# Attention decode over a cached K and V: the V loads move from SyncE's DMA queue to ScalarE's

## The chip, the cores and the metric

The kernel runs on one core of one Trainium2 chip. Five engines of the core follow their own instruction streams and meet through semaphores: TensorE (PE; its weight loads are shown as PEld), VectorE (DVE), ScalarE (ACT), GpSimd (POOL) and SyncE (SP). Transfers between HBM and the on-chip memory SBUF run on 16 DMA engines. An engine issues a transfer onto its own DMA queue and goes on; the transfer raises a semaphore when it has landed. The metric is the device time of one execution in microseconds (us), lower is better.

## The reference

One token per sequence (two sequences, D = 512) passes a block that adds a gated attention to its input. Only the parts that carry the time are kept here:

```python
xn = _layernorm(x)
q = (xn @ wq).reshape(B, 1, 32, 128)                 # 32 query heads
k = repeat(k_cache, 4, axis=1)                       # caches: (2, 8, 32768, 128), float32
v = repeat(v_cache, 4, axis=1)
p = softmax(einsum("bhqd,bhkd->bhqk", q, k) * 128 ** -0.5)
s = einsum("bhqk,bhkd->bhqd", p, v).reshape(B, 1, 4096) @ wo
gate, up = xn @ W_gate, xn @ W_up                    # 512 x 1792
g = silu(((gate * (gate > 0)) * up) @ W_down)
return x + s * g
```

K and V are 268 MB each, and every byte of them is read once. All arithmetic is float32.

## The kernel before

The 16 groups (a sequence and one of its 8 K/V heads, with 4 query heads each) have 32768 tokens each. A tile `t` is 8192 tokens, four tiles make a group, and two tiles make a pair. There are 64 tiles and 32 pairs (`PAIRS`). One transfer brings one pair of K or of V: 128 partitions of 64 KB, 8.39 MB.

Three large buffers of SBUF hold everything that is loaded. `kbuf[0]` and `kbuf[1]` (`k0`, `k1`) take the K pairs in turn. `wide` (shown as `w`) takes first `wq`, then the gate and up weights, then the down weights, and then one V pair after the other. So K is held twice and V once. At the end the V of pair 30 goes to `k0`, and `wo` to `k1` in six pieces.

The main loop (line 882) runs over steps `j` from 0 to 33. In step `j`

- DVE turns the K of pair `j` in place, in eight instructions (`k_transpose`, L660), and PE follows it with the scores (`scores`, tile `s`);
- PE sums the V of pair `j - 2` with its softmax weights (`values`, tile `o`);
- DVE takes the scores out of PSUM (`take_scores`, L678);
- in an odd step a group ends: its maximum is found and ScalarE takes the exponentials of its four tiles (`maximum`, L722); the group two steps back is divided by its sum and stored (`sums`, `take_o`, `finish_group`);
- PE and DVE bring the weights of pair `j - 1` into the layout for the next step's sums (`weights`, tile `pt`, and `take_weights`, L737);
- last, the step's loads are issued: the V of pair `j - 1`, then the K of pair `j + 2`.

All loads but two tiny ones go through `load` (L239) on SyncE, in this order, so its queue holds V, K, V, K in turn. The order of an engine's instructions is the order in which the program is written. `Program.op` works out the waits from the keys that an operation reads and writes: a load has to wait until the last reader of its buffer is done. For a V load that is the `values` call of the same step; for a K load it is the `scores` call of the same step. SyncE meets the V load first, so the K load behind it is issued when the sums over V are done too, although its own buffer is free since the scores.

ScalarE, VectorE and TensorE run the steps from 4 to 64 tiles as a hardware loop whose body is four tiles long (`looped`, L86); a body has to be the same in all rounds. ScalarE's body holds the four exponentials. SyncE's and GpSimd's programs are written out.

Of the kernel before, what the change touches and what calls it, by code (L numbers as in the profile page):

```python
# [162 lines left out]
def decode_block_kernel(nc, x, kc, vc, wq, wo, wg, wu, wd, out):  # L163
# [5 lines left out]
    NU = SK // TK  # L169
    NG = B * HKV  # L170
    NK = NG * NU
# [5 lines left out]
    PAIRS = NK // 2  # L177

    pg = Program()

    def sbuf(name, *shape, align=32):
        return nc.alloc_sbuf_tensor(name, list(shape), F32, align_bytes=align)[:]
# [5 lines left out]
    wide = sbuf("w", P, 2 * NC * NR * DH, align=ALIGN)  # L188
# [47 lines left out]
    def pe(fn, r=(), w=()):  # L236
        pg.op("PE", fn, r, w)

    def load(dst, src, sem, r=(), w=(), engine="SP"):  # L239
        pg.op(engine, lambda e: e.dma_start(dst, src), r, w, dma=sem)  # L240

    def mm(out_, lhs, rhs, start, stop):
        return lambda e: e.matmul(out_, lhs, rhs, start=start, stop=stop, skip_group_check=True)  # L243

    def chain(parts):
        def emit(e):
            for f in parts:
                got = f(e)
            return got

        return emit

    def group(g):
        return g % B, g // B
# [42 lines left out]
    for kb in range(4):  # L297
        dve(
            lambda e, kb=kb: e.memset(block_of[Q * kb : Q * kb + Q, kb * REP : (kb + 1) * REP], 1.0),
            w=["block_of"],  # L300
# [105 lines left out]
    def k_keys(b):  # L406
        return [f"k{b}"] + [f"k{b}_{i}_{c}" for i in range(2) for c in range(NC)]

    def load_kk(j):
        b = j % 2  # L410
        load(kbuf[b], rows_of(kc, 2 * j), f"k{b}", w=k_keys(b))

    def rows_of(src, t):
        b, hk = group(t // NU)
        lo = (t % NU) // 2 * 2 * TK
        return src[b, hk, lo : lo + 2 * TK, :].rearrange("(p r) d -> p (r d)", p=P)
# [6 lines left out]
    def place(t):  # L423
        if t in (NK - 4, NK - 3):
            return half_of(kbuf[0], t), "k0"
        return half_of(wide, t), "wide"

    def load_vv(j):
        if 2 * j == NK - 4:
            load(kbuf[0], rows_of(vc, 2 * j), "k0", w=k_keys(0))  # L430
        else:
            load(wide, rows_of(vc, 2 * j), "v", w=["wide"])

    def in_halves(tokens):
        return tokens.rearrange("p (h c r d) -> p h c r d", h=2, c=NC, d=DH)
# [3 lines left out]
    def load_wo():  # L439
        for quad, cuts in enumerate(((0, 16), (0, 8, 12, 14, 15, 16))):  # L440
            dst = kbuf[1][:, quad * ROWS * D : (quad + 1) * ROWS * D]
            WO.append(dst.rearrange("p (j d) -> p j d", j=ROWS))
            n = ROWS * P
            rows = wo[quad * n : (quad + 1) * n, :].rearrange("(p j) d -> p (j d)", j=ROWS)
            for lo, hi in zip(cuts, cuts[1:]):
                name = f"wo{quad}_{lo}"
                for j in range(lo, hi):
                    WOK[quad, j] = name
                load(
                    dst[:, lo * D : hi * D],  # L450
                    rows[:, lo * D : hi * D],
                    name,
                    w=[*k_keys(1), name] if quad == 0 else [name],
                )
# [71 lines left out]
    def take_query(g):  # L526
        b, hk = group(g)
        pg.op(
            "POOL",
            lambda e: e.tensor_tensor(  # L530
                qcur.rearrange("p e (k h) -> p e k h", h=REP),
                qall[:, b, hk].unsqueeze(2).to_broadcast([P, 4, Q // REP, REP]),
                block_of.rearrange("p (k h) -> p k h", h=REP)
                .unsqueeze(1)
                .to_broadcast([P, 4, Q // REP, REP]),
                op=ALU.mult,
            ),
            ["qall", "block_of"],
            ["qcur", "pool"],
        )  # L540
# [61 lines left out]
    def load_d():  # L602
        load(
            wide[:, : FI * D],
            wd.rearrange("(p i) d -> p (i d)", p=P),
            "wd",
            w=["wide", "wide_g", "wide_u"],
        )

    def mlp_down():  # L610
        ht = wt[1][:, : FI * Q].rearrange("p (i m) -> p i m", m=Q)
        pe(
            chain(
                [
                    mm(
                        ps_d[32 * (i % 4) : 32 * (i % 4) + 32, :],
                        ht[:, i, :],
                        wdt[:, i, :],
                        i < 4,
                        i >= FI - 4,  # L620
                    )
                    for i in range(FI)
                ]
            ),
            ["wt1", "wide"],
            ["d"],
        )
# [29 lines left out]
    def k_transpose(t, c):  # L657
        at_, key = turned(t, c)
        at_ = at_.rearrange("p h r d -> p h (r d)")
        dve(lambda e: e.transpose(at_, at_), [f"k{t // 2 % 2}"], [key])  # L660

    def scores(t):
        ps = ps_s[t % 2]

        def one(e, c):
            part = turned(t, c)[0].rearrange("p h r (e k) -> p h r e k", e=4)
            return mm(ps[Q * c : Q * c + Q, :], qcur[:, e, :], part[:, :, :, e, :], e == 0, e == 3)

        for c in range(NC):
            pe(one(0, c), [turned(t, c)[1], "qcur"], [f"s{t % 2}"])  # L670
        pe(chain([one(e, c) for e in (1, 2) for c in range(NC)]), ["qcur"], [f"s{t % 2}"])
        for c in range(NC):
            pe(one(3, c), [turned(t, c)[1], "qcur"], [f"s{t % 2}"])
# [62 lines left out]
    def take_weights(t):  # L736
        dve(lambda e: e.transpose(wt[t % 2], ps_p[t % 2]), [f"pt{t % 2}"], [f"wt{t % 2}"])  # L737

    def values(t):
        u = t % NU  # L740
        at_, key = place(t)
        w = wt[t % 2].rearrange("p (r m) -> p r m", m=Q)

        def one(r):
            a = Q * (r % 4)
            return mm(
                o_ps[a : a + NC * REP, :].rearrange("p (c d) -> p c d", c=NC),
                w[:, r, : NC * REP],
                in_halves(at_)[:, r // 8, :, r % 8, :],
                u == 0 and r < 4,  # L750
                u == NU - 1 and r >= NR - 4,
            )

        pe(chain([one(r) for r in range(NR)]), [f"wt{t % 2}", key], ["o"])
# [93 lines left out]
    def project_far():  # L848
# [25 lines left out]
            ["gy"],  # L874
        )

    load_kk(0)
    project_q()
    load_gu()
# [2 lines left out]
    for j in range(PAIRS + 2):  # L882
        s, v = 2 * j, 2 * (j - 2)
        pg.step = s
        live, summed, ends = j < PAIRS, v >= 0, j % 2
        if live:
            for t in (s, s + 1):
                for c in range(NC):
                    k_transpose(t, c)
                scores(t)  # L890
                if t == 2:
                    mlp_down()
            if ends and j + 1 < PAIRS:
                take_query(j // 2 + 1)
        if j == 0:
            mlp_gu("g", 0)
            mlp_gu("u", 1)
        if summed:
            values(v)
            values(v + 1)  # L900
        if live:
            take_scores(s)
            take_scores(s + 1)
        if j == 0:
            mlp_vector()
        if j == 1:
            mlp_fold()
        if ends:
            if live:
                tile_maximum()  # L910
            if summed:
                sums()
            if live:
                maximum()
            if summed:
                take_o()
                if not live:
                    project_near(range(2))
                finish_group(j // 2 - 1)
        if 0 <= v + 2 < NK:  # L920
            for t in (v + 2, v + 3):
                weights(t)
                take_weights(t)
        if j == 0:
            load_d()
        elif j < PAIRS - 1:
            load_vv(j - 1)
        if j == PAIRS - 2:
            load_vv(PAIRS - 2)
        if j + 2 < PAIRS:  # L930
            load_kk(j + 2)
        if j == PAIRS - 1:
            load_vv(PAIRS - 1)
            load_wo()

    project_near(range(2, NEAR))
    project_far()
# [2 lines left out]
    sems = {s: nc.alloc_semaphore(f"sem_{s}") for s in pg.count}  # L940
    with nc.Block(no_gpsimd_drain=True) as block:

        @block.sync
        def _(e):
            pg.emit("SP", e, sems)

        @block.scalar
        def _(e):
            pg.emit("ACT", e, sems, loop=(NU, NK))

        @block.gpsimd
        def _(e):
            pg.emit("POOL", e, sems)

        @block.vector
        def _(e):
            pg.emit("DVE", e, sems, loop=(NU, NK))

        @block.tensor
        def _(e):  # L960
            pg.emit("PE", e, sems, loop=(NU, NK))
# [34 lines left out]
```

## Time and profile before

| | before |
|---|---|
| median of 3 runs | 1309.91 us (1309.86 to 1310.29) |
| span of the profiled execution, first to last instruction | 1308.4 us |
| read from HBM | 564.67 MB, 432 GB/s over the span |
| TensorE busy | 859.0 us (66%) |
| VectorE busy | 718.1 us (55%) |
| ScalarE busy | 51.4 us (4%) |
| transfers of K and V | 32 + 32, of 8.39 MB |

The median is 1.5 us above the span of the profiled execution. A row of the timeline gives start, duration, engine, line, operation, output and input, and in brackets how long the engine had been idle and what ended that. `SPq` and `ACTq` are the DMA queues' issuing instructions. A row by windows gives, for a stretch of time, the busy time of each engine, then the clock that TensorE was granted, the mean busy share of the 16 DMA engines, and the rate in GB/s.

### The profile page before, as it was taken

The page shows a single profiled execution, that of the slowest core. Times are in us where ns is not written, and L with a number is a line of the kernel's source. Part 1 is how long each engine was busy: PE and PEld are TensorE (multiplying, and loading weights), DVE is VectorE, ACT ScalarE, POOL GpSimd, SP SyncE. Part 2 cuts the span into 40 slices and gives each one's busy share as a digit, 9 for nine tenths or more (in the row PEclk, how much of TensorE's full clock was granted, in tenths as well). Part 3 has the DMA queues.
Part 4 walks back from the last instruction along what each step waited for, and adds up shares of the span by engine and source line. Part 5 has one row for each costly group of instructions (what it writes and reads, how often), then busy time and mean ns, then how long its engine had stood idle before and what let it go on. Part 6 is the DMA issues. An engine that isn't in the chain of part 4 may idle for free.

```text
span 1308.4 us, 11146 instructions
## 1 busy us (share of the span) xinstructions
PE 859.0 (66%) x4720; PEld 211.5 (16%) x4720; DVE 718.1 (55%) x690; ACT 51.4 (4%) x133; POOL 10.5 (1%) x38
## 2 busy tenths in 40 slices
PE   3566675785666587576667667667665757865676
PEld 1111111211111121111111112121111112111121
DVE  3566654565655456664546666455665545656521
ACT  0001000000000000000000000000000000000000
POOL 0000000000000000000000000000000000000000
PEclk9677788878878887878898778798887889788788
DMA  9999999999999999999999999999999999999998
GB/s 417 423 438 435 437 431 441 425 439 429 437 429 439 435 433 441 429 441 427 439 429 437 429 439 435 433 441 429 441 427 439 429 437 429 439 435 433 439 431 357
DMA packets 10693, 564.79 MB, mean 432 GB/s; under 512 B 1195, under 2 KB 1211, under 8 KB 1597
## 3 DMA queue, kind: packets, MB, share of 16 engines
q1 hardware_dynamic: 10668, 564.67, 99.7%
q8 instruction: 6, 0.10, 0.0%
q14 instruction: 3, 0.02, 0.0%
q10 hardware_dynamic: 16, 0.01, 0.0%
HBM read 564.67 MB, written 0.00 MB: 432 GB/s over the span
## 4 chain that ended last, share of the span: by engine, by line
DMA 64%; DVE 17%; PE 15%; issue 4%; SPq 0%
DMA k<-in_A_k_cache_dram 58%; DVE k L660 17%; PE o L243 8%; PE s L243 6%; DMA k<-in_A_wo_dram 3%; DMA w<-in_A_wq_dram 2%; PE m_ps L243 1%; PE m_ps L693 0%; PE d L243 0%; SPq L240 0%; DVE gy L870 0%; DVE gy L872 0%
## 5 line engine op out<-in xcount | busy, mean ns | idle before, releaser
L243 PE MATMUL s<-k,qcur 128*32 128x512 f32 x2048 | 504.5, 710 | 370.5 <-DVE k L660 370.3
L660 DVE STREAM_TRANSPOSE k<-k 128x2048 f32<-128x2048 f32 x256 | 565.2, 2275 | 147.0 <-DMA k<-in_A_k_cache_dram 147.0
L243 PE MATMUL o<-w,wt 128*16 128x512 f32 x1984 | 245.5, 596 | 9.0 <-DMA w<-in_A_v_cache_dram 9.0
L243 PEld LDWEIGHTS s<-k,qcur 128*32 128x32 f32 x2048 | 89.5, 123 | 785.0 <-DVE k L660 639.3
L737 DVE STREAM_TRANSPOSE wt<-pt 128x512 f32<-128x512 f32 x64 | 45.9, 717 | 139.4 <-PE pt L243 134.6
L678 DVE TENSOR_SCALAR_CACHE_REDUCE st<-s 128x512 f32<-128x512 f32 x64 | 43.0, 672 | 120.9 <-PE s L243 120.9
L243 PEld LDWEIGHTS o<-w,wt 128*16 128x16 f32 x1984 | 62.4, 98 | 167.5 <-issue 167.5
L722 ACT ACTIVATE st<-st,nb 128x512 f32<-128x512 f32 x64 | 45.4, 710 | 1111.0 <-DVE nb L719 1111.0
L243 PE MATMUL pt<-st,perm 128*128 128x512 f32 x128 | 72.6, 696 | 1.5 <-ACT st L722 1.5
L763 DVE RECIPROCAL rl<-m_ps 128x1 f32<-128x1 f32 x16 | 2.7, 169 | 111.0 <-PE m_ps L243 111.0
L243 PE MATMUL m_ps<-ob,heads 128*128 128x128 f32 x128 | 21.7, 321 | 29.0 <-DVE ob L777 29.0
L243 PEld LDWEIGHTS pt<-st,perm 128*128 128x128 f32 x128 | 25.3, 219 | 34.4 <-issue 30.1
L803 DVE STREAM_TRANSPOSE os<-m_ps 128x512 f32<-128x512 f32 x16 | 11.5, 717 | 23.2 <-PE m_ps L243 23.2
L243 PEld LDWEIGHTS m_ps<-ob,heads 128*128 128x128 f32 x128 | 18.0, 217 | 31.1 <-DVE ob L777 31.1
L243 PE MATMUL m_ps<-w,wt 128*32 128x512 f32 (+1 forms) x128 | 16.2, 640 | 8.1 <-DMA w<-in_A_wq_dram 8.1
L777 DVE SCALAR_TENSOR_TENSOR ob<-o,share,ob 128x128 f32<-128x128 f32 x48 | 16.9, 351 | 1.7
L530 POOL TENSOR_TENSOR qcur<-qall,block_of 128x128 f32<-128x128 f32 x16 | 6.5, 406 | 1008.3 <-PE s L243 974.0
L243 PE MATMUL m_ps<-negone,mrow 1*128 1x1 f32 x32 | 6.0, 256 | 9.3 <-DVE mrow L708 9.3
L722 ACT ACTIVATION_READ_ACCUMULATOR st<-st,nb 128x1 f32 x64 | 11.9, 186 | 0.0
L481 DVE COPY os<-m_ps 128x512 f32<-128x512 f32 x2 | 1.4, 692 | 16.3 <-PE m_ps L243 16.3
L243 PE MATMUL o<-k,wt 128*16 128x512 f32 x64 | 8.4, 687 | 2.8 <-DMA k<-in_A_v_cache_dram 2.8
L391 PE MATMUL m_ps<-ident,st 32*128 32x32 f32 x4 | 0.7, 307 | 14.0 <-DVE st L380 14.0
(80 smaller groups left out, 102.8 us busy)
## 6 DMA issues: line engine op xcount, KB each, us to landing
k<-in_A_wo_dram SPq DMA_DIRECT2D x1, 4096.0 KB, 37.3
w<-in_B_W_gate_dram SPq DMA_DIRECT2D x1, 3584.0 KB, 19.6
w<-in_B_W_up_dram SPq DMA_DIRECT2D x1, 3584.0 KB, 27.6
w<-in_B_W_down_dram SPq DMA_DIRECT2D x1, 3584.0 KB, 15.6
k<-in_A_wo_dram SPq DMA_DIRECT2D x1, 2048.0 KB, 41.7
k<-in_A_wo_dram SPq DMA_DIRECT2D x1, 1024.0 KB, 43.7
k<-in_A_k_cache_dram SPq DMA_DIRECT2D x32, 48.2
k<-in_A_wo_dram SPq DMA_DIRECT2D x1, 512.0 KB, 44.5
```

Source lines behind the costliest of these rows:

```text
L243: return lambda e: e.matmul(out_, lhs, rhs, start=start, stop=stop, skip_group_check=True)
L391: lambda e, k=k: e.transpose(px[:, k * 32 : (k + 1) * 32], xquad[:, k, :], ident[:32, :32])
L481: dve(lambda e, q=qs, h=half: e.tensor_copy(q, pq[h]), [f"m{half}"], [f"os{half}"])
L530: lambda e: e.tensor_tensor(qcur.rearrange("p e (k h) -> p e k h", h=REP), qall[:, b, hk].unsqueeze(2).to_broadcast([P, 4, Q // REP, REP]) ...
L660: dve(lambda e: e.transpose(at_, at_), [f"k{t // 2 % 2}"], [key])
L678: lambda e: e.tensor_scalar(st[u], ps_s[t % 2], SCALE, None, op0=ALU.mult, op1=ALU.max, accum_out=mx[:, u : u + 1],),
L722: lambda e, u=u: e.activation(st[u], st[u], AF.Exp, bias=nb, scale=1.0, accum_out=ls[:, u : u + 1]),
L737: dve(lambda e: e.transpose(wt[t % 2], ps_p[t % 2]), [f"pt{t % 2}"], [f"wt{t % 2}"])
L763: dve(lambda e: e.reciprocal(rl, ps_m[1][:, :1]), ["m1"], ["rl"])
L777: lambda e, part=part, c=c: e.scalar_tensor_tensor(ob, part, share[:, c : c + 1], ob, op0=ALU.mult, op1=ALU.add),
L803: lambda e: e.transpose(ot, ps_m[1].rearrange("p (h q j) -> p j h q", h=REP, j=ROWS)),
```

## The change

The function `load_vv` issues its transfer from ScalarE, except for the V of pair 30, which goes into `k0` and stays on SyncE. All loads of a step are gathered in `load_next`, and its call stands directly behind the sums over V instead of at the step's end. ScalarE therefore waits for the sums, issues the V load, and then comes to the exponentials of the step. Since its instructions no longer repeat in equal rounds, its program is written out in full.

```diff
-            load(wide, rows_of(vc, 2 * j), "v", w=["wide"])
+            load(wide, rows_of(vc, 2 * j), "v", w=["wide"], engine="ACT")
...
+    def load_next(j):
+        if j == 0:
+            load_d()
+        elif j < PAIRS - 1:
+            load_vv(j - 1)
+        if j == PAIRS - 2:
+            load_vv(PAIRS - 2)
+        if j + 2 < PAIRS:
+            load_kk(j + 2)
+        if j == PAIRS - 1:
+            load_vv(PAIRS - 1)
+            load_wo()
...
         if summed:
             values(v)
             values(v + 1)
+        load_next(j)
         if live:
             take_scores(s)
             take_scores(s + 1)
...
-        if j == 0:
-            load_d()
-        elif j < PAIRS - 1:
-            load_vv(j - 1)
-        if j == PAIRS - 2:
-            load_vv(PAIRS - 2)
-        if j + 2 < PAIRS:
-            load_kk(j + 2)
-        if j == PAIRS - 1:
-            load_vv(PAIRS - 1)
-            load_wo()
...
-            pg.emit("ACT", e, sems, loop=(NU, NK))
+            pg.emit("ACT", e, sems)
```

SyncE at the end of the main loop before: the last K pair, the last three V pairs and the first pieces of `wo`. A bracket names what an instruction waits for, and no bracket means no wait of its own.

```order
L240 DMA k1<-in_A_k_cache_dram 128x16384
L240 DMA w<-in_A_v_cache_dram 128x16384 [waits sem_PE]
L240 DMA k0<-in_A_v_cache_dram 128x16384
L240 DMA w<-in_A_v_cache_dram 128x16384 [waits sem_PE]
L240 DMA k1<-in_A_wo_dram 128x8192
L240 DMA k1<-in_A_wo_dram 128x4096
```

SyncE at the same place now:

```order
L240 DMA k0<-in_A_k_cache_dram 128x16384 [waits sem_PE]
L240 DMA k1<-in_A_k_cache_dram 128x16384 [waits sem_PE]
L240 DMA k0<-in_A_v_cache_dram 128x16384 [waits sem_PE]
L240 DMA k1<-in_A_wo_dram 128x8192 [waits sem_PE]
L240 DMA k1<-in_A_wo_dram 128x4096
```

The V loads into `w` are gone from SyncE. The K loads, the V of pair 30 and `wo` have a wait of their own now, for the scores that were the last to read their buffer.

ScalarE from the last exponential of the first group on, before (the loop's body stands between the two branches):

```order
L722 ACTIVATE st3,ls<-st3,nb 128x512
L144 UNCONDITIONAL_BRANCH
L722 ACTIVATE st0,ls<-st0,nb 128x512 [waits sem_DVE]
L722 ACTIVATE st1,ls<-st1,nb 128x512
L722 ACTIVATE st2,ls<-st2,nb 128x512
L722 ACTIVATE st3,ls<-st3,nb 128x512
L156 ISA
L144 COMPARE_AND_BRANCH
```

ScalarE at the same place now (`x2` stands for two V loads, of an even and of the next odd step, each with its own wait):

```order
L722 ACTIVATE st3,ls<-st3,nb 128x512
L240 DMA w<-in_A_v_cache_dram 128x16384 [waits sem_PE] x2
L722 ACTIVATE st0,ls<-st0,nb 128x512 [waits sem_DVE]
L722 ACTIVATE st1,ls<-st1,nb 128x512
L722 ACTIVATE st2,ls<-st2,nb 128x512
L722 ACTIVATE st3,ls<-st3,nb 128x512
```

Between the exponentials of two groups stand two V loads, so the exponentials of a group come behind the V load of their own step. TensorE, VectorE and GpSimd keep their order.

## The prediction

> **What bounds the kernel now.** I read the page first (busy shares, the row of DMA shares, the chain), then the windows, then two steps of the timeline in the middle.
>
> ```profile
> PE 859.0 (66%) x4720; PEld 211.5 (16%) x4720; DVE 718.1 (55%) x690; ACT 51.4 (4%) x133; POOL 10.5 (1%) x38
> DMA  9999999999999999999999999999999999999998
> GB/s 417 423 438 435 437 431 441 425 439 429 437 429 439 435 433 441 429 441 427 439 429 437 429 439 435 433 441 429 441 427 439 429 437 429 439 435 433 439 431 357
> DMA packets 10693, 564.79 MB, mean 432 GB/s; under 512 B 1195, under 2 KB 1211, under 8 KB 1597
> DMA 64%; DVE 17%; PE 15%; issue 4%; SPq 0%
> ```
> ```profile
> 0.00:50.00 50.00, 16.71 (x96) 6.29 (x96) 17.66 (x45) 2.86 (x3) 1.10 (x7) 0.87 0.98 416
> 300.00:600.00 300.00, 204.95 (x1105) 49.35 (x1105) 174.05 (x158) 11.71 (x32) 2.44 (x8) 0.82 1.00 434
> ...
> 1258.00:1304.00 46.00, 30.90 (x215) 9.56 (x213) 8.30 (x22) 2.93 (x8) 0.42 (x2) 0.85 0.97 417
> ```
>
> The last two columns are the reading that matters: the DMA engines have a busy share of 1.00 at 434 GB/s through the main loop, and 0.97 to 0.98 at the ends. No compute engine is over 66%. The kernel is bound by bytes, and it holds that bound because the DMA engines never lack a queued transfer. Whatever the change does, there is next to nothing to gain, and every microsecond in which the queues run empty is lost. So the question is how full the queues stay. These are two steps from the timeline, an odd one and the even one after it, and one row of the chain for the sums of the odd one:
>
> ```profile
> 600.09 0.33 SPq L240 DMA_DIRECT2D w<-in_A_v_cache_dram  x1
> 600.46 0.43 SPq L240 DMA_DIRECT2D k<-in_A_k_cache_dram  x1
> 601.15 1.57 DVE L737 STREAM_TRANSPOSE wt<-pt 128x512 f32<-128x512 f32 x2 [7.22 <-PE pt L243]
> 609.77 17.66 DVE L660 STREAM_TRANSPOSE k<-k 128x2048 f32<-128x2048 f32 x8 [7.04 <-DMA k<-in_A_k_cache_dram]
> 639.70 0.33 SPq L240 DMA_DIRECT2D w<-in_A_v_cache_dram  x1
> 640.07 0.44 SPq L240 DMA_DIRECT2D k<-in_A_k_cache_dram  x1
> 644.94 1.58 DVE L737 STREAM_TRANSPOSE wt<-pt 128x512 f32<-128x512 f32 x2
> 648.43 17.66 DVE L660 STREAM_TRANSPOSE k<-k 128x2048 f32<-128x2048 f32 x8 [1.92 <-DMA k<-in_A_k_cache_dram]
> 676.67 0.33 SPq L240 DMA_DIRECT2D w<-in_A_v_cache_dram  x1
> 687.04 4.50 DVE L660 STREAM_TRANSPOSE k<-k 128x2048 f32<-128x2048 f32 x2 [7.74 <-DMA k<-in_A_k_cache_dram]
> ```
> ```profile
> 632.80 6.87 PE o L243 x61
> ```
>
> The K pairs land at 609.8, 648.4 and 687.0, 38.6 us apart. Two loads move in that time, so a load alone takes 19.3 us. At 600.1, when V and K are issued, the K pair before them still needs 9.7 us. V then follows and lands near 629, and K at 648.4. That is the order in which they are used: the sums over V start at 632.8, 4 us after V is there. V is wanted soonest, because it has one buffer, and one queue serves it first.
>
> From these rows I take the compute times. From K's arrival to the end of the sums it takes 29.9 us in the odd step (609.77 to 639.70) and 28.2 in the even one (648.43 to 676.67), 29.1 in the mean. The sums are 6.9 of that (632.80 row), so turning and scores are 22.2. After the sums DVE is free for the next K after 6.8 us in an odd step (639.70 to 646.52) and after 2.6 in an even one (600.09 to 602.72).
>
> **The change part by part.** *Issue and ScalarE.* 31 V issues go from SyncE to ScalarE. There they stand ahead of the exponentials, which have this room (timeline, waits, and the queue of instruction fetches):
>
> ```profile
> 1.42 1.19 ACTq L240 DMA_DIRECT2D st<-in_A_x_dram  x1
> 2.66 0.60 ACTq L240 DMA_DIRECT2D xy<-in_A_x_dram  x1
> 641.18 0.72 ACT L722 ACTIVATE st<-st,nb 128x512 f32<-128x512 f32 x1 [76.04 <-DVE nb L719]
> ```
> ```profile
> ACT st L722 <- DVE nb L719: 1111.0, 15, 76.0
> ```
> ```profile
> q8 instruction: 6, 0.10, 0.0%
> ```
>
> The exponentials start 1.48 us after the sums end (639.70 to 641.18), and an issue on ScalarE took 0.60 and 1.19 us in the two cases seen. It fits; at worst 0.3 us in each of 15 odd steps would be lost if that cover went. I take 0. The written-out program replaces a loop on an engine that is idle for 76 us at a time; instruction fetches moved 0.1 MB before, so even ten times that is 2 us of DMA. I take 0 here too. The code's place in the step changes nothing on PE, DVE or POOL, whose order stays.
>
> *The K load comes loose.* On SyncE it no longer queues behind the V load's wait. It goes out when the scores end, 6.9 us before the sums do. That alone cannot speed up full DMA engines, but it gives K a head start.
>
> *Two queues.* How do they share? The trace has one case, at the start (timeline, and the chain's row for wq):
>
> ```profile
> 0.74 0.39 SPq L240 DMA_DIRECT2D w<-in_A_wq_dram  x1
> 1.19 0.41 SPq L240 DMA_DIRECT2D k<-in_A_k_cache_dram  x1
> ...
> 10.13 0.68 DVE L364 TENSOR_REDUCE stat<-st 32x1 f32<-32x512 f32 x1 [2.91 <-DMA st<-in_A_x_dram]
> ```
> ```profile
> 0.74 21.90 DMA w<-in_A_wq_dram
> ```
>
> The 4 KB of x, issued on ScalarE's queue at 1.42, were there at 10.1, while SyncE's 8.39 MB of wq, issued before them, landed at 22.6 with K behind. So the queues interleave. But x took 8.7 us, so it was not put first either: it waited its turn among large pieces. Leaving out the packets under 2 KB, 9482 packets carry 564.7 MB, 60 KB each; a full 64 KB row at 434/16 GB/s is 2.4 us. I take equal shares, packet by packet. A transfer on an empty queue has 2.6 us of latency (21.9 less 19.3); I put half ahead of it and half behind.
>
> The Trainium skill, DMA: Bandwidth & Descriptors, section Queues, rings and completion order, says that each DMA engine goes round robin between the queues that have work, a packet at a time. The x row agrees with that, and no row here shows it for two long transfers.
>
> Now the loop with equal shares. *Even step, counted from the odd step's V issue:* when V starts at 1.3, r us of K's work are left. Both are through at 1.3 + 19.3 + r = 20.6 + r. The scores end at 6.8 + 22.2 = 29.0; until then both K buffers are full and V's waits for the sums behind those scores, so nothing is queued. The next K moves from 29.0 + 1.3 = 30.3. The DMA engines are idle for 9.7 - r. The sums end at 29.0 + 6.9 = 35.9, and V is issued. *Odd step, counted from there:* when V starts (1.3), K has had 6.9 us alone and has 12.4 left. Sharing, it needs 24.8 and ends at 26.1. The scores end at 2.6 + 22.2 = 24.8 and send the next K, which moves from 26.1. V still has 19.3 - 12.4 = 6.9 to go, shares again, ends at 26.1 + 13.8 = 39.9 and lands at 41.2. PE waits 16.4 us for it. The sums behind such a wait take 8.7 (tail, below), so they end at 49.9. K had 6.9, and 11.3 alone until the next V starts, so r = 19.3 - 18.2 = 1.1. Idle time is 9.7 - 1.1 = 8.6 per two steps, which now take 35.9 + 49.9 = 85.8 instead of 77.2. Since the second half does not depend on r, this sets in at once and repeats. Even steps 6 to 30 are 13; step 4 I count as running in. 13 x 8.6 = 111.8.
>
> *The end.* Before, in the timeline and the chain's last row:
>
> ```profile
> 1257.88 0.33 SPq L240 DMA_DIRECT2D w<-in_A_v_cache_dram  x1
> 1266.75 8.43 PE L243 MATMUL o<-k,wt 128*16 128x512 f32 x64 [2.81 <-DMA k<-in_A_v_cache_dram]
> 1286.06 9.01 PE L243 MATMUL o<-w,wt 128*16 128x512 f32 x64 [8.97 <-DMA w<-in_A_v_cache_dram]
> 1302.97 0.16 PEld L243 LDWEIGHTS s<-k,ots 128*32 128x32 f32 x8 [1.38 <-DMA k<-in_A_wo_dram]
> 1304.21 0.38 PEld L243 LDWEIGHTS s<-k,ots 128*32 128x32 f32 x16 [1.08 <-DMA k<-in_A_wo_dram]
> ```
> ```profile
> 1306.28 0.29 DVE gy L872
> ```
>
> The last V landed at 1286.1 and wo behind it at 1304.2, with 2.4 us of work left (to 1306.6, where the last row ends). Now wo, on SyncE, starts before that V and is done first; V lands last. Behind it come its sums (8.7, between 8.43 and 9.01) and the end from 1295.1 to 1306.6, 11.5 less the two waits for wo of 1.38 and 1.08, so 9.0. That is 17.7 in place of 2.4: +15.3.
>
> *Sum:* span 1308.4 + 111.8 + 15.3 = 1435.5, and the median stands 1.5 above the span: 1437. Bounds of this case: if the sums take 6.9 behind a wait too, r is 2.9, the idle 6.8, the end 13.5, and the time 1309.9 + 88.4 + 13.5 = 1412. If a landing waits for one more packet of the other queue (2.4 us), the pair takes 10.9 more: 1309.9 + 141.7 + 15.3 = 1467.
>
> **The rivals.** *V is served soon enough:* if shares favour V, it lands 21.9 after its issue, ahead of the scores in both halves (24.8 and 29.0), and K always has work for the rest; the DMA engines stay full. Then only the end costs. If V shares with 8.9 us of the V in k0 (1257.9 to 1266.8) and then with wo, it lands at 1257.9 + 19.3 + 19.3 = 1296.5 and the end at 1314.2: +7.6; at most +15.3. That is 1318 to 1325, slower. The x row's 8.7 us speaks against favour for ScalarE's queue, but x is small.
> *V is starved:* with one third, V ends 6.9 us later in the odd half, and the pair costs about 15.4: 1309.9 + 200 + 15 = 1525. Nothing speaks for it.
> *Faster, by rate:* two queues could keep the DMA engines at the best slice's rate. The page's best slices show 441 GB/s against 432; 564.7 MB would take 1280 instead of 1308, so 1282. It decides where the rate gain exceeds the idle time, but a busy share of 1.00 with one queue leaves no gaps to fill.
> *Nothing happens:* the same 564.67 MB move at 434 GB/s, the order does not matter and only issue time moves: 1310. It needs the last V ahead of wo and no empty queue.
> The Trainium skill, DMA: Bandwidth & Descriptors, section Issuing engines are not separate DMA queues, says that issuing from several engines saves only the sequencer's time, as all run on the same 16 DMA engines. By that rule alone this rival would hold.
>
> **How the numbers follow.** Equal shares with idle time: 0.66, 1437 (1412 to 1467). V soon enough: 0.17. Starved: 0.07. Faster: 0.05. Nothing: 0.05. About 0.2% is what a measurement of this kernel can tell from no change, so faster 0.05, same 0.05, slower 0.90. The range from 1317 to 1467 takes in the first two cases; starved, faster and nothing lie outside, and with the uncertainty inside the first case that leaves 2 in 10.
>
> **What would show it.** Right: the DMA share in the middle falls to about 0.90 and the rate to 390 GB/s; V issues on ScalarE alternate at 36 and 50 us; wo lands before the last V; and of these two waits of before, PE's for V becomes some 14 x 16 = 220 us and DVE's for K, one per step, mostly vanishes.
>
> ```profile
> DVE k L660 <- DMA k<-in_A_k_cache_dram: 147.0, 31, 7.7
> ...
> PE o L243 <- DMA w<-in_A_v_cache_dram: 9.0, 1, 9.0
> ```
>
> Wrong: a share that stays 1.00 in the middle means V was served in time (look at the end for 8 to 15 us); steps of equal length with idle engines mean that the shares are not equal; exponentials later than 2 us after the sums mean the issue on ScalarE is dear.

## The result and the profile after

The changed kernel is slower: 1438.7 us against 1310.0 in the longest comparison (median of six executions), 1469.1 in the first one (median of four). The ratio is 1.098 (95% interval 1.096 to 1.099) in the longest and 1.104 (1.099 to 1.108) in the first. Its executions fall into two groups, near 1438 us and near 1485 us with a lower granted clock (one, of 1454.5, lies between); the ratios are of the quicker group, and the profile of the changed kernel is of the slower one.

So the loop is read below from a kernel that differs from the changed one only in the last V load (the last experiment below). Its profiled execution has a span of 1432.9 us at a granted clock of 0.82. First the page of the changed kernel itself, with the chain that ended last by engine and by line:

```profile
PE 895.1 (60%) x4720; PEld 225.5 (15%) x4720; DVE 714.8 (48%) x690; ACT 51.4 (3%) x133; POOL 10.5 (1%) x38
DMA  9999997979699797988979799797988979699793
DMA 49%; PE 28%; DVE 21%; issue 2%; DVEq 0%; SPq 0%
DMA w<-in_A_v_cache_dram 44%; DVE k L660 18%; PE o L243 17%; DMA k<-in_A_k_cache_dram 6%; PE s L243 4%; PE pt L243 3%; PE m_ps L243 3%; DVE ob L777 1%; DVE ob L771 0%; DVE share L766 0%; PE m_ps L693 0%; DVE mr L698 0%; DVE mrow L708 0%; DVE wt L737 0%; DVE rl L763 0%
```

The same chain by line before:

```profile
DMA k<-in_A_k_cache_dram 58%; DVE k L660 17%; PE o L243 8%; PE s L243 6%; DMA k<-in_A_wo_dram 3%; DMA w<-in_A_wq_dram 2%; PE m_ps L243 1%; PE m_ps L693 0%; PE d L243 0%; SPq L240 0%; DVE gy L870 0%; DVE gy L872 0%
```

The two waits in the changed kernel that the prediction named:

```profile
PE o L243 <- DMA w<-in_A_v_cache_dram: 271.6, 16, 20.4
...
DVE k L660 <- DMA k<-in_A_k_cache_dram: 21.1, 3, 8.0
```

And the middle of the loop by windows, first before, then the kernel that differs from the changed one in the last V load:

```profile
300.00:1200.00 900.00, 597.40 (x3214) 144.49 (x3218) 516.71 (x471) 35.14 (x96) 7.33 (x24) 0.83 1.00 434
```
```profile
300.00:1200.00 900.00, 544.55 (x2960) 125.44 (x2960) 467.04 (x425) 29.29 (x80) 6.50 (x21) 0.83 0.92 392
```

The row of 9s has broken: the DMA engines were busy all the time and now are for 0.92 of it, and the rate fell from 434 to 392 GB/s. The clock is the same, 0.83. PE used to wait 9 us for V in the whole execution, now 272; DVE's wait for K, 147 us before, is 21. The chain that ended last goes through the V loads now (44% of the span), and went through the K loads before (58%). The same bytes move, at the wrong times: K is there early, V late.

One pair of steps in that kernel's timeline:

```profile
575.73 0.34 ACTq L240 DMA_DIRECT2D w<-in_A_v_cache_dram  x1
...
599.62 54.94 SPq L240 DMA_DIRECT2D k<-in_A_k_cache_dram  x2
...
617.45 8.68 PE L243 MATMUL o<-w,wt 128*16 128x512 f32 x64 [17.86 <-DMA w<-in_A_v_cache_dram]
...
626.20 0.33 ACTq L240 DMA_DIRECT2D w<-in_A_v_cache_dram  x1
...
627.64 0.72 ACT L722 ACTIVATE st<-st,nb 128x512 f32<-128x512 f32 x1 [82.43 <-DVE nb L719]
...
632.90 17.62 DVE L660 STREAM_TRANSPOSE k<-k 128x2048 f32<-128x2048 f32 x8
...
653.61 7.45 PE L243 MATMUL o<-w,wt 128*16 128x512 f32 x61
...
661.10 0.33 ACTq L240 DMA_DIRECT2D w<-in_A_v_cache_dram  x1
```

The V issued at 575.7 is used at 617.4, after 41.7 us, and PE has waited 17.9 us for it. The V issued at 626.2 is there when the scores are done; its sums start at 653.6 without a wait. DVE starts on K as soon as it is free (632.9, no wait behind the row), since K has long landed. The two halves are 50.5 and 34.9 us, 85.4 in all, where two steps took 77.2 before.

### The profile page after: what moved, and what is told of

Its sections match the earlier page's. It is cut to its first block, busy times and chain, and to the rows that moved or that the text cites. A ratio compares the mean times of both kernels' runs of the same rounds, so it can differ in the third digit from the quotient of the medians.

```text
span 1484.7 us, 11114 instructions
## 1 busy us (share of the span) xinstructions
PE 895.1 (60%) x4720; PEld 225.5 (15%) x4720; DVE 714.8 (48%) x690; ACT 51.4 (3%) x133; POOL 10.5 (1%) x38
## 3 DMA queue, kind: packets, MB, share of 16 engines
q1 hardware_dynamic: 6204, 304.62, 48.0%
## 4 chain that ended last, share of the span: by engine, by line
DMA 49%; PE 28%; DVE 21%; issue 2%; DVEq 0%; SPq 0%
DMA w<-in_A_v_cache_dram 44%; DVE k L660 18%; PE o L243 17%; DMA k<-in_A_k_cache_dram 6%; PE s L243 4%; PE pt L243 3%; PE m_ps L243 3%; DVE ob L777 1%; DVE ob L771 0%; DVE share L766 0%; PE m_ps L693 0%; DVE mr L698 0%; DVE mrow L708 0%; DVE wt L737 0%; DVE rl L763 0%
## 5 line engine op out<-in xcount | busy, mean ns | idle before, releaser
L243 PE MATMUL s<-k,qcur 128*32 128x512 f32 x2048 | 472.9, 664 | 251.1 <-DVE k L660 250.3
L243 PE MATMUL o<-w,wt 128*16 128x512 f32 x1984 | 272.2, 683 | 271.6 <-DMA w<-in_A_v_cache_dram 271.6
L243 PEld LDWEIGHTS s<-k,qcur 128*32 128x32 f32 x2048 | 85.2, 119 | 646.4 <-DVE k L660 514.6
L243 PE MATMUL pt<-st,perm 128*128 128x512 f32 x128 | 89.0, 834 | 1.5 <-ACT st L722 1.5
L243 PE MATMUL m_ps<-ob,heads 128*128 128x128 f32 x128 | 32.3, 432 | 29.2 <-DVE ob L777 29.2
L243 PEld LDWEIGHTS pt<-st,perm 128*128 128x128 f32 x128 | 30.0, 258 | 38.9 <-issue 36.8
L243 PEld LDWEIGHTS m_ps<-ob,heads 128*128 128x128 f32 x128 | 27.7, 319 | 31.4 <-DVE ob L777 31.4
L243 PE MATMUL m_ps<-w,wt 128*32 128x512 f32 (+1 forms) x128 | 16.4, 645 | 8.1 <-DMA w<-in_A_wq_dram 8.1
L243 PEld LDWEIGHTS m_ps<-w,wt 128*32 128x32 f32 x128 | 6.0, 122 | 17.1 <-issue 17.1
## 6 DMA issues: line engine op xcount, KB each, us to landing
w<-in_B_W_gate_dram SPq DMA_DIRECT2D x1, 3584.0 KB, 19.3
```

## The experiments

### Without the new queue

All of the change stays except the queue:

```diff
-            load(wide, rows_of(vc, 2 * j), "v", w=["wide"], engine="ACT")
+            load(wide, rows_of(vc, 2 * j), "v", w=["wide"])
```

> The change without its new queue: the loads are written behind the sums and ScalarE's program is written out, but V stays on SyncE. Equal-shares theory (the loss comes from V and K sharing the DMA engines): the queue holds V, K, V, K as before, so 1310, within 3 us. Rival (the place of the loads or the written-out program costs): 1400 or more.

Measured: 1310.0 us, ratio 1.000 (0.999 to 1.001). Neither the place of the loads in the program nor ScalarE's written-out program costs anything. The whole loss hangs on the queue of the V loads.

### Two queues, old order

Each V and each K load is cut in two, tile by tile. One half goes to each queue, V ahead of K on both, and a K load waits for the sums as it did before (`due` names an operation to wait for without reading its tile):

```diff
-        load(kbuf[b], rows_of(kc, 2 * j), f"k{b}", w=k_keys(b))
+        for i, q in enumerate(("SP", "ACT" if j > 2 else "SP")):
+            load(
+                kbuf[b][:, i * HALF : (i + 1) * HALF],
+                rows_of(kc, 2 * j)[:, i * HALF : (i + 1) * HALF],
+                f"k{b}h{i}",
+                w=[f"k{b}h{i}"] + [f"k{b}_{i}_{c}" for c in range(NC)],
+                engine=q,
+                due=["o"] if j > 2 else [],
+            )
...
-            load(wide, rows_of(vc, 2 * j), "v", w=["wide"], engine="ACT")
+            for i, q in enumerate(("SP", "ACT" if j else "SP")):
+                load(
+                    wide[:, i * HALF : (i + 1) * HALF],
+                    rows_of(vc, 2 * j)[:, i * HALF : (i + 1) * HALF],
+                    f"v{i}",
+                    w=[f"wideh{i}"] if j else ["wide", f"wideh{i}"] if i == 0 else [f"wideh{i}"],
+                    engine=q,
+                    due=["o"],
+                )
```

> Two queues, old order: every V and K load is cut in two halves, one on SyncE and one on ScalarE, V ahead of K on both, all issued when the sums end. Equal-shares theory: the two halves of V share with each other and K stays behind them, so the DMA engines stay full and the time is 1310 to 1315. Rival (a second long stream lowers the rate, or issues on ScalarE cost by themselves): 1400 or more, with a DMA share below 1.00 or a rate below 430 GB/s.

Measured: 1313.4 us, ratio 1.003 (1.002 to 1.004). By windows:

```profile
300.00:1200.00 900.00, 600.73 (x3196) 144.86 (x3196) 512.14 (x469) 35.17 (x96) 7.35 (x24) 0.82 1.00 433
```

Two long streams side by side move 433 GB/s at a share of 1.00, and ScalarE issues nearly twice as many transfers as in the changed kernel. So a second queue is not slow, and issuing from ScalarE is not dear. What the change lost is the order: V first, then K.

### K without its head start

```diff
-        load(kbuf[b], rows_of(kc, 2 * j), f"k{b}", w=k_keys(b))
+        load(kbuf[b], rows_of(kc, 2 * j), f"k{b}", w=k_keys(b), due=["o"])
```

> The changed kernel, but a K load waits for the sums like the V load, so K's head start of 6.9 us is gone; V on ScalarE, K on SyncE. Equal-shares theory: V and K then move together for 38.6 us, V lands 41.2 after its issue in every step, the sums end at 49.9, and the queues are empty for 11.3 us of each step: 29 steps x 11.3 = 328, so about 1640. Rival (the head start is what does the harm, since it puts K ahead of V): back towards 1310.

Measured: 1668.9 us, ratio 1.274 (1.271 to 1.276), 29 us more than expected. The middle by windows, the times from issue to landing of the V loads from 300 to 1400 us (the view of the tile `w`), and the sums of one step:

```profile
300.00:1200.00 900.00, 503.09 (x2437) 119.26 (x2429) 392.74 (x360) 26.37 (x72) 5.51 (x18) 0.74 0.78 331
```
```profile
DMA to landing us min/median/max: 41.1/41.4/42.6
```
```profile
649.58 9.55 PE L243 MATMUL o<-w,wt 128*16 128x512 f32 x64 [11.14 <-DMA w<-in_A_v_cache_dram]
```

V and K set out together and share to the end: V lands after 41.4 us (41.2 expected) in every step, and then the queues are empty until the sums are done. Those sums take 9.55 us instead of 8.7, at a granted clock of 0.74; over 29 steps that is some 25 of the 29 us above the expectation. So beside a V load on another queue the head start does no harm but helps: in the changed kernel it fills part of the time in which V is not moving, and without it the loss is 2.8 times as large, the lower clock included. The rival falls.

### K in two and in four pieces

K is cut into loads of 32 KB or 16 KB rows on SyncE; V keeps its 64 KB rows, and the instructions that turn K wait for all of its pieces (the loads are shown, for two pieces):

```diff
-        load(kbuf[b], rows_of(kc, 2 * j), f"k{b}", w=k_keys(b))
+        cut = 2 * NC * NR * DH // 2
+        for i in range(2):
+            load(
+                kbuf[b][:, i * cut : (i + 1) * cut],
+                rows_of(kc, 2 * j)[:, i * cut : (i + 1) * cut],
+                f"k{b}p{i}",
+                w=[*k_keys(b), f"k{b}p0"] if i == 0 else [f"k{b}p{i}"],
+            )
```

> The changed kernel with each K load cut into two transfers of 32 KB rows on SyncE; V stays whole with 64 KB rows on ScalarE. If the DMA engines take turns packet by packet, V gets two thirds of the rate while both move, lands about 31 us after its issue, and most of the idle time goes: 1330 to 1360. Rival (shares are equal in bytes): as the changed kernel, 1437 to 1487.

Measured: 1366.4 us, ratio 1.042 (1.040 to 1.044), a little above the range.

> The changed kernel with each K load cut into four transfers of 16 KB rows, V whole. Turns packet by packet: V gets four fifths while both move and lands about 27 us after its issue, before or with the scores, so faster again than two pieces (1366): 1325 to 1350. Rival (two pieces helped by something else, such as K's first half landing early): no further gain, 1360 to 1370.

Measured: 1338.3 us, ratio 1.024 (1.020 to 1.027). The V loads from issue to landing, with two pieces and with four:

```profile
DMA to landing us min/median/max: 27.8/31.6/33.5
```
```profile
DMA to landing us min/median/max: 27.9/28.3/28.7
```

A load alone takes 19.3 us and 2.6 of latency. With K's rows as long as V's, V lands after 41.4, and 2.6 + 19.3 x 2 is 41.2. With rows of one half it lands after 31.6 in the median: 2.6 + 19.3 x 3/2 is 31.6 (27.8 where K was through early). With a quarter, 28.3: 2.6 + 19.3 x 5/4 is 26.7. So V's part of the rate is 1/2, about 2/3 and about 3/4. The queues do not share by bytes; turns row by row give the first two landings, and with four pieces V gets less than the 4/5 that they would give. Why is open. The profile counts a row as one packet: SyncE's queue moves the same 304.62 MB in 6204 packets in the changed kernel, in 10812 with two pieces and in 20028 with four. The middle of the loop with four pieces shows that the engines stay full again:

```profile
300.00:1200.00 900.00, 617.41 (x3219) 149.96 (x3211) 501.78 (x456) 32.21 (x88) 7.11 (x23) 0.81 1.00 431
```

The Trainium skill, DMA: Bandwidth & Descriptors, section Queues, rings and completion order, says that an engine goes round robin between queues and changes only at packet boundaries. The landings beside whole and halved K loads agree with it for two long transfers, if a row of up to 64 KB counts as the packet; the one beside quarters comes 1.6 us later than it would give.

### V in two pieces

The opposite cut, on ScalarE's loads, with K whole:

```diff
-            load(wide, rows_of(vc, 2 * j), "v", w=["wide"], engine="ACT")
+            cut = NC * NR * DH
+            for i in range(2):
+                load(
+                    wide[:, i * cut : (i + 1) * cut],
+                    rows_of(vc, 2 * j)[:, i * cut : (i + 1) * cut],
+                    f"v{i}",
+                    w=["wide"] if i == 0 else ["wide_1"],
+                    engine="ACT",
+                )
```

> The opposite: V is cut into two transfers of 32 KB rows on ScalarE, K stays whole. Turns packet by packet: V gets one third while both move, lands later than in the changed kernel, and the time rises: 1500 to 1610. Rival (any cut helps, or shares are equal in bytes): 1437 to 1487 or less.

Measured: 1526.3 us, ratio 1.163 (1.158 to 1.167), and in the middle, with the landings of V's halves:

```profile
300.00:1200.00 900.00, 494.70 (x2667) 117.42 (x2659) 421.13 (x384) 26.36 (x72) 5.88 (x19) 0.79 0.85 364
```
```profile
DMA to landing us min/median/max: 11.9/24.0/48.6
```

Cutting as such does not help; whose rows are longer decides. The prediction's rival with a starved V had V land 6.9 us later than 41.2, at 48.1, and put its price at 1525; here V's second half lands after 48.6 at the latest.

### Only the last V

```diff
-            load(wide, rows_of(vc, 2 * j), "v", w=["wide"], engine="ACT")
+            load(wide, rows_of(vc, 2 * j), "v", w=["wide"], engine="ACT" if j == PAIRS - 1 else "SP")
```

> Only the V load of the last pair goes to ScalarE; all others stay on SyncE. Equal-shares theory: the last V shares with the V in k0 and with wo and lands some 10 us later (1296.5 instead of 1286), wo lands at the same time as before: 1318, between 1315 and 1325. Rival (the end hides it): 1310.

Measured: 1315.0 us, ratio 1.004 (1.002 to 1.005): 5 us, at the low end. Its timeline:

```profile
1257.86 0.36 ACTq L240 DMA_DIRECT2D w<-in_A_v_cache_dram  x1
...
1273.87 8.40 PE L243 MATMUL o<-k,wt 128*16 128x512 f32 x64 [9.96 <-DMA k<-in_A_v_cache_dram]
...
1293.23 8.96 PE L243 MATMUL o<-w,wt 128*16 128x512 f32 x64 [9.04 <-DMA w<-in_A_v_cache_dram]
...
1312.23 0.29 DVE L872 TENSOR_TENSOR gy<-gy,xy 128x128 f32<-128x128 f32 x1
```

The V in k0 is 7.1 us later than before (1273.9 against 1266.8) and the last V 7.2 later (1293.2 against 1286.1). I had reckoned 10.4 for the last V with equal shares all the way; but the first piece of wo that it meets besides has rows of 32 KB, and by the cut loads above V gets two thirds against those. That fits the smaller delay; it was not tried by itself.

### K ahead of V on one queue

Everything on SyncE, and `load_next` calls `load_kk` before `load_vv`:

```diff
-            load(wide, rows_of(vc, 2 * j), "v", w=["wide"], engine="ACT")
+            load(wide, rows_of(vc, 2 * j), "v", w=["wide"])
...
-        elif j < PAIRS - 1:
+        if j + 2 < PAIRS:
+            load_kk(j + 2)
+        if 0 < j < PAIRS - 1:
             load_vv(j - 1)
         if j == PAIRS - 2:
             load_vv(PAIRS - 2)
-        if j + 2 < PAIRS:
-            load_kk(j + 2)
```

> One queue, SyncE, but the K load stands ahead of the V load and goes out when the scores end: the head start without sharing. If V is late because K is ahead of it, V waits in the odd half for 12.4 us of K, lands at 34.3 instead of 41.2, and the pair costs 1.7 us; with V landing last at the end (+15) that is 1350, between 1340 and 1375. Rival (only sharing of two queues does harm): 1310 to 1325.

Measured: 1350.5 us, ratio 1.033 (1.030 to 1.036), the number I had written, though not for its reasons. In this kernel the last V still stands ahead of wo, so the 15 us of the end do not arise, and the loop loses more than I had reckoned:

```profile
300.00:1200.00 900.00, 597.75 (x3151) 140.54 (x3151) 496.60 (x451) 32.23 (x88) 6.70 (x22) 0.83 0.99 423
```

423 instead of 434 GB/s is 2.6%, some 30 us of the loop, where 1.7 us a pair, some 22, had been reckoned. Still it separates the two things: K ahead of V on one queue costs 40 us, and the two queues that share cost 128.

### The changed kernel again

> The changed kernel once more, for a profile beside which the steps of the working can be laid, and for the spread of its time (1437 to 1487 so far). If the clock that TensorE is granted explains the spread, then a span near 1437 goes with a clock near 0.82 and one near 1485 with 0.78, and what differs inside a pair of steps is the closing work of an odd step and the sums behind a wait (9.3 and 9.6 us in the profile at 0.778), while V's landing stays 41 to 42 us after its issue. Rival (the sharing of the queues varies): V's landing differs between the profiles.

> The changed kernel once more, for a profile at the clock of its quicker runs (0.82). If TensorE's clock makes the difference of 47 us between 1438 and 1485, the closing of an odd step (from the V issue to DVE's next turn) takes some 7 us instead of 9.3, the sums behind a wait 8.7 instead of 9.6, and V lands 41 to 42 us after its issue as before. Rival (the queues share otherwise): the landing is what differs.

Measured: 1438.7 us, ratio 1.098 (1.096 to 1.099), and 1439.7 us, ratio 1.097 (1.096 to 1.099). Both profiles came at clocks of 0.77 and 0.78, so the working can be laid only beside the kernel shown above, at 0.82. V's longest time to landing is 41.8 and 41.7 us in these two and 41.7 there; the sums behind a wait take 9.6 us in the first profile of the changed kernel and 8.7 there, and the closing of an odd step 9.3 and 6.7. The rival falls: the shares of the queues are the same. What sets the clock was not tried.

### The last V back on SyncE

Once in the changed kernel and once with K in four pieces:

```diff
-            load(wide, rows_of(vc, 2 * j), "v", w=["wide"], engine="ACT")
+            load(wide, rows_of(vc, 2 * j), "v", w=["wide"], engine="SP" if j == PAIRS - 1 else "ACT")
```

> The changed kernel with the V load of the last pair alone back on SyncE, ahead of wo, which is then issued with it. The prediction charged the end 15.3 us for V landing last: by that, 1438 becomes 1423. Rival (the order at the end moves bytes only from one side of the last V to the other, since wo had already moved while PE waited): wo then lands some 20 us behind the last V, and the time stays between 1433 and 1442.

Measured: ratio 1.095 (1.093 to 1.097), beside 1.097 (1.096 to 1.099) for the changed kernel in the same comparison: some 3 us less, with intervals that overlap.

> K in four pieces as before (1338), and the V load of the last pair alone goes back to SyncE, where it stands ahead of wo. The prediction's price for the end is 15.3 us, so 1323, between 1320 and 1330. Rival (the end costs less than that here, as in the run with only the last V moved, which lost 5): 1332 to 1336.

Measured: 1332.3 us, ratio 1.018 (1.015 to 1.020), 6 us less than 1338.3, whose ratio lies between 1.020 and 1.027: hardly clear of the spread.

Both rivals hold. These are the two ends in the timeline, first of the changed kernel, then with the last V back on SyncE:

```profile
1414.49 2.85 SPq L240 DMA_DIRECT2D k<-in_A_wo_dram  x6
...
1462.98 9.57 PE L243 MATMUL o<-w,wt 128*16 128x512 f32 x64 [6.78 <-DMA w<-in_A_v_cache_dram]
...
1482.58 0.29 DVE L872 TENSOR_TENSOR gy<-gy,xy 128x128 f32<-128x128 f32 x1
```
```profile
1387.04 0.33 SPq L240 DMA_DIRECT2D w<-in_A_v_cache_dram  x1
...
1387.41 2.98 SPq L240 DMA_DIRECT2D k<-in_A_wo_dram  x6
...
1409.01 8.84 PE L243 MATMUL o<-w,wt 128*16 128x512 f32 x64 [7.02 <-DMA w<-in_A_v_cache_dram]
...
1428.71 0.38 PEld L243 LDWEIGHTS s<-k,ots 128*32 128x32 f32 x16 [1.10 <-DMA k<-in_A_wo_dram]
...
1430.81 0.29 DVE L872 TENSOR_TENSOR gy<-gy,xy 128x128 f32<-128x128 f32 x1
```

In the changed kernel V lands last and 19.9 us of work follow. With V ahead, wo lands 19.7 us behind the last V and little follows, but wo has not moved while PE waited for the V before, so the bytes are still to come.

The windows show it: from the last V issue to the end, first before, then in the changed kernel; then, in the changed kernel and with the last V back on SyncE, the two steps ahead of the last V issue; and last, with V back, from there to the end:

```profile
1257.90:1308.39 50.49, 32.72 (x255) 10.57 (x254) 9.57 (x25) 2.93 (x8) 0.42 (x2) 0.86 0.89 382
1438.40:1484.65 46.25, 33.90 (x255) 11.81 (x254) 9.57 (x25) 2.93 (x8) 0.42 (x2) 0.85 0.53 229
1353.10:1438.40 85.30, 54.25 (x280) 13.38 (x279) 43.63 (x40) 2.93 (x8) 0.20 (x1) 0.78 0.87 368
1308.80:1387.00 78.20, 51.37 (x278) 11.80 (x278) 43.64 (x40) 2.93 (x8) 0.20 (x1) 0.85 0.77 331
1387.00:1432.89 45.89, 31.18 (x255) 10.33 (x254) 9.58 (x25) 2.93 (x8) 0.42 (x2) 0.93 0.87 366
```

From the last V issue on, the DMA engines stand idle for some 6 us before and 22 in the changed kernel. With V back on SyncE it is 6 again, but 18 instead of 11 in the two steps ahead. So much of what is saved at the end is lost ahead of it. The rows of the two kernels come at different clocks, so they do not add up to the 3 us.

## Why the prediction was right

**The bound.** It held: with a share of 1.00 there was nothing to win, and the loss is the time in which the queues are empty. In the middle of the loop I had announced a share of about 0.90 and 390 GB/s; 0.92 and 392 came.

**Issue and ScalarE, both taken as 0.** Right. The first experiment shows it for the place and the written-out program. A V issue on ScalarE took 0.33 to 0.36 us, and the exponentials come 1.44 us after the V issue (626.20 to 627.64).

**Equal shares.** Right, and it was the step on which all rested, taken from one 4 KB transfer. V lands 41.7 us after its issue in the half in which K shares all the way (41.2 in the working), and cutting the rows moves the landing as turns row by row make it, but for the 1.6 us with four pieces. The shares are equal because K and V both have rows of 64 KB, as the prediction's "packet by packet" has it.

**The pair of steps.** The halves are 34.9 and 50.5 us for 35.9 and 49.9, the pair 85.4 for 85.8; the sums behind a wait 8.68 for 8.7, the closing of an odd step 6.7 for 6.8, turning and scores 21.3 (632.9 to 654.2) for 22.2, PE's wait 17.9 for 16.4. That is 8.2 more per pair. Over the 14 pairs of the loop it makes 115 of the 128 us; the prediction had 13 x 8.6 = 112, so that a slightly large term and one pair too few cancel, which is luck. PE's waits for V come to 266.7 us in that kernel, where some 220 were forecast: 14 of about 17.7, and two more at the end, of 10.4 and 7.0, that the forecast did not count.

**The end, 15.3 us.** It holds for the changed kernel: the V lands last, 19.9 us of work follow in place of 2.4, and the DMA engines stand idle for some 16 us more behind the last V issue. The 13 us that the 14 pairs leave of the loss fit too. As a price of the last V by itself it was wrong: moved alone, the last V costs 5 us (the rival with V served in time had put 7.6 to 15.3), and moved back it saves 3 to 6, hardly clear of the spread.

**The rivals.** That V is served soon enough, and that nothing happens, fall with the landings; so does a starved V, which would land after 48.1 us and not 41.7. No version moved more than the 434 GB/s of before in the middle, so nothing was faster by rate. By the Trainium skill, DMA: Bandwidth & Descriptors, section Issuing engines are not separate DMA queues, several issuing engines only save issue time. Here nothing was saved and 9.8% were lost. As to rate the measurement agrees with it (433 GB/s with two queues, 434 with one); what the sentence leaves out is the order that one queue keeps.

**Sum.** 1437 predicted, 1438.7 and 1439.7 measured in the longer comparisons. The median of the first, 1469.1, lies 2 us above the stated range; the sum has no term for TensorE's clock.

None of the versions tried beats the kernel before. The best with two queues keeps the old order and takes 1313.

## What to carry to other kernels

Where the DMA engines are full, one queue is also a schedule: it says which buffer is filled first. Before splitting a stream over two queues, ask which transfer is wanted first and which buffer is single, and work out when that one lands if it gets half the rate. If two queues have to be used, give the urgent transfer the longer rows, or put pieces of everything on both queues in the same order.

## What the runs showed of the hardware that I had not expected

- Two queues share by rows of the transfer rather than by bytes: V landed after 41.4, 31.6 and 28.3 us beside K rows of 64, 32 and 16 KB. Row length thus works as a priority: cutting K's rows alone took the changed kernel from 1438 to 1338 us.
- A transfer that starts earlier can be worth much even where the DMA engines are the bound: taking 6.9 us of head start from K cost another 230 us (1438.7 to 1668.9), because the two streams then start and end together; the granted clock was lower too (0.74).
- Two queues with 32 KB rows moved 433 GB/s, one with 64 KB rows 434: the second queue itself is all but free.
